# Experts: high parts first in one output column, scatters of a slot together and without order among slots, weight pieces that subtract a PSUM copy

## The chip, the cores and the metric

The kernel runs on one core of a Trainium2 chip. The metric is the device time of one execution in microseconds. TensorE multiplies into PSUM, VectorE and ScalarE split, copy and transpose, GpSimd splits and issues the indirect DMAs, SyncE issues the plain ones.

## The reference

An attention over 8 batches, 8 heads, 576 positions of 64, and behind it a mixture of experts. With `x` the 4608 x 512 rows that the attention gives:

```python
g_idx = np.argmax(x @ w_group, axis=1)             # one of 4 groups
e_idx = np.argmax(xg @ w_expert[g], axis=1)        # one of 4 experts in it
h  = np.maximum(xg[mask_e] @ w1[g, e], 0.0)        # 512 -> 1024
ye = h @ w2[g, e]                                  # 1024 -> 512
out[tok_idx] = combined[:, None] * ye              # combined: product of two softmax weights
```

Each row goes to one of 16 experts, so the rows of `out` that two experts write are distinct.

## The kernel before, in words

The first half of the time (up to about 480 us) is the attention and the routing. The change lies in the second, `moe`. The 16 experts are put in order of their counts and each gets a **slot** of fixed capacity, `CAPS` = 384, 368, 344, 332, 322, 314, 306, 300, 294, 288, 284, 280, 272, 264, 256, 256. Slot 0 is cut into 256 rows and a tile of 128 (`rest`). What doesn't fit is done behind a branch that isn't taken here.

A product in single precision is made of three: every operand is split into a high part in the type fp32r and a low part, the difference, and `h*h`, `h*l` and `l*h` are added in PSUM. So weights have `wh` and `wl`, the input `xh` and `xl`, the hidden rows `hh` and `hl`.

For slots 1 to 15 the loop at the end of `moe` writes the order of TensorE, VectorE and ScalarE out by hand; GpSimd's and SyncE's order is left to a scheduler. In slot k it does:

- **h part**, 8 items (`h_items`): 12 matmuls into one of four accumulators in PSUM, then on ScalarE `hh` (relu), then on VectorE `hl` = max(ph, 0) - hh. Behind item i stands one Z item of the slot before and weight piece i of the slot after.
- **y part**, 4 items (`y_items`), one for each 128 output columns: 24 matmuls, and on ScalarE a copy of the column into `yT`. Ahead of item i stand four X items, two weight pieces and one Z item.

The three lists that are woven in:

- **W**, 16 weight pieces of 128 x 512 of the next slot (`load`): ScalarE makes `wh` from `raw`, then `wl` = raw - wh on VectorE (pieces 0, 4, 8, 10, 12, 14) or on GpSimd (the other ten).
- **X**, the next slot's input (`x_items`): eight items of two VectorE transposes each from `xg` to `xt`, then two that make `xh` (ScalarE) and `xl` (VectorE).
- **Z**, the rows of the slot before (`z_items`): eight items of two VectorE transposes from `yT` to `yr`, then for each 128 rows a `leave`: ScalarE scales the rows by `cw`, GpSimd scatters them to `out` with an indirect DMA. There is one buffer `yr`, so the transposes of a slot into `yr` wait until the scatters of the slot before have landed.

Slots 14 and 15 have a capacity that 128 divides; they multiply straight into rows (`y_rows`) and have no Z of their own. The PSUM pool `pt` has four buffers of 512 columns; in the loop nothing uses it. The weave of the y part is this line:

```python
run(X[4 * i:4 * i + 4] + W[8 + 2 * i:10 + 2 * i] + Z[8 + i:9 + i])
```

so the three `leave`s stand in y items 0, 1 and 2.

## Time and profile before

| | |
|---|---|
| median of 3 runs | 1027.92 us (1026.99 to 1028.95) |
| the profiled execution | 1027.76 us |
| its span, first to last instruction | 1025.7 us |
| busy share of the span: TensorE, VectorE, ScalarE, GpSimd | 88%, 74%, 55%, 55% |
| slots 2 to 13 | 583.4 to 956.6 us |
| mean granted share of TensorE's clock | 0.949 |

Busy shares are averages over parts with different limits; a busy TensorE is not TensorE at its peak. An engine does its instructions in the order of its queue, and the idle time ahead of an instruction is put down to what ended it. A releaser is inferred from semaphores. Line numbers (L953) are those of the kernel before.

### The profile page before, as it was taken

Reading aid. Unit: us, or ns where it says so; the run is one execution under the profiler, and the core shown is the slowest. Engines: PE = TensorE matmul, PEld = TensorE weight load, DVE = VectorE, ACT = ScalarE, POOL = GpSimd, SP = SyncE. Lnnn points to the kernel's source line nnn. Section 1 sums busy time; section 2 is a strip of 40 time slices with the busy share of each in tenths; the row PEclk is TensorE's granted clock in tenths of the full one; section 3 lists DMA queues with packets and bytes.
Section 4 is the critical chain, followed back from the end, with each engine's and each line's share of the span. In section 5 each row is a group of like instructions: output and inputs, shape, how many; then the busy total and the mean of one; then the engine's idle time right before and its main releaser. Section 6 shows DMA issues by size and latency. Waiting matters only on the chain.

```text
span 1025.7 us, 17682 instructions
## 1 busy us (share of the span) xinstructions
PE 900.0 (88%) x5640; PEld 805.6 (79%) x5640; DVE 759.3 (74%) x2023; ACT 569.0 (55%) x1298; POOL 559.6 (55%) x682
## 2 busy tenths in 40 slices
PE   4888999979999999997497999999988998998984
PEld 3777877868788787875387998898888888887873
DVE  7456676866968787866728898878978779888870
ACT  4557675766767676775153454555545454455530
POOL 8434453554636355436277566666656575666630
PEclk9999998999999999998788999999989999999997
DMA  7999999999979899732156444544444544455410
GB/s 201 248 213 235 238 237 224 225 222 225 253 187 247 221 231 226 196 128 68 73 218 200 175 150 164 200 175 149 170 160 163 204 154 158 166 196 193 147 39 21
DMA packets 64164, 187.22 MB, mean 183 GB/s; under 512 B 9628, under 2 KB 18460, under 8 KB 55872
## 3 DMA queue, kind: packets, MB, share of 16 engines
q1 hardware_dynamic: 54768, 166.76, 59.0%
q0 software_dynamic: 7488, 18.89, 5.0%
q8 instruction: 46, 0.75, 0.3%
q10 hardware_dynamic: 1808, 0.37, 0.2%
q14 instruction: 54, 0.44, 0.1%
HBM read 112.12 MB, written 19.69 MB: 129 GB/s over the span
## 4 chain that ended last, share of the span: by engine, by line
PE 52%; DVE 25%; DMA 14%; issue 5%; ACT 2%; POOL 0%; SPq 0%; ACTq 0%; POOLq 0%; DVEq 0%
PE py L1100 12%; PE po L297 11%; PE ph L1045 10%; DVE yr L1138 6%; PE pm L201 4%; DVE wl L953 4%; PE ps L257 4%; PE ps L259 4%; DVE xt L1012 4%; DMA WA<-tl 4%; DVE hl L1041 3%; DMA out_dram<-yr,ids 3%; DMA VT<-in_v_dram 3%; DMA WA<-hl 2%; DVE mx L209 2%
## 5 line engine op out<-in xcount | busy, mean ns | idle before, releaser
L953 POOL TENSOR_TENSOR wl<-raw,wh 128x512 fp32r<-128x512 f32 x166 | 215.9, 1321 | 85.2 <-ACT wh L950 45.0
L209 DVE CUSTOM_DVE_ANT_0 mx<-pm,mask 128x192 bf16<-128x192 f32 (+4 forms) x320 | 127.8, 419 | 63.1 <-PE pm L201 60.7
L1045 PE MATMUL ph<-xh,wh 128*128 128x256 f32 (+13 forms) x512 | 150.3, 312 | 24.3 <-DVE hl L1041 21.1
L950 ACT CAST wh<-raw 128x512 fp32r<-128x512 f32 x256 | 148.1, 616 | 13.4 <-DMA raw<-in_w_dram 13.4
L1045 PE MATMUL ph<-xl,wh 128*128 128x256 f32 (+13 forms) x512 | 149.2, 310 | 1.9 <-DVE xl L1017 1.7
L1100 PE MATMUL py<-hl,wh 128*128 128x256 f32 (+13 forms) x448 | 133.0, 315 | 19.0 <-DVE hl L1041 18.9
L257 PE MATMUL ps<-WA 68*128 68x320 f32 (+4 forms) x384 | 138.7, 365 | 7.7 <-DMA WA<-tl 3.3
L201 PE MATMUL pm<-WA 66*128 66x288 f32 (+4 forms) x384 | 127.8, 364 | 19.2 <-DMA WA<-ch 10.9
L297 PE MATMUL po<-pt,VT 128*128 128x256 f32 (+3 forms) x512 | 125.5, 363 | 17.1 <-DMA VT<-in_v_dram 5.8
L1100 PE MATMUL py<-hh,wh 128*128 128x256 f32 (+13 forms) x448 | 130.8, 310 | 6.3 <-ACT wh L950 6.3
L1138 DVE STREAM_TRANSPOSE yr<-yT 32x384 f32<-32x384 f32 (+1 forms) x208 | 104.6, 503 | 39.4 <-DMA out_dram<-yr,ids 35.2
L1045 PEld LDWEIGHTS ph<-xh,wh 128*128 128x128 f32 x512 | 100.9, 197 | 28.3 <-DVE hl L1041 23.9
L1040 ACT ACTIVATE hh<-ph 128x256 fp32r<-128x256 f32 (+13 forms) x128 | 53.5, 418 | 122.0 <-PE ph L1045 121.3
L276 POOL TENSOR_SCALAR_AFFINE_SELECT pt<-pt 128x128 f32<-128x128 f32 (+2 forms) x192 | 63.7, 339 | 102.9 <-ACT pt L267 99.8
L297 PEld LDWEIGHTS po<-pt,VT 128*128 128x128 f32 x512 | 89.4, 196 | 33.8 <-issue 12.6
L259 PE MATMUL ps<-WB 128*128 128x320 f32 (+4 forms) x384 | 112.3, 305 | 0.0
L1012 DVE STREAM_TRANSPOSE xt<-xg 32x256 f32<-32x256 f32 (+1 forms) x224 | 109.5, 489 | 3.4
L297 PE MATMUL po<-pu,VT 128*128 128x320 f32 (+1 forms) x384 | 109.3, 394 | 0.0
L1100 PEld LDWEIGHTS py<-hl,wh 128*128 128x128 f32 x448 | 87.8, 196 | 25.9 <-DVE hl L1041 25.9
L1045 PEld LDWEIGHTS ph<-xl,wh 128*128 128x128 f32 x512 | 100.9, 197 | 3.7 <-DVE xl L1017 3.0
L953 DVE TENSOR_TENSOR wl<-raw,wh 128x512 fp32r<-128x512 f32 x90 | 90.2, 1004 | 15.2 <-ACT wh L950 13.7
L359 POOL TENSOR_TENSOR xTl<-xT,xTh 128x512 fp32r<-128x512 f32 x30 | 38.2, 1274 | 110.8 <-ACT xTh L355 99.5
(236 smaller groups left out, 1979.6 us busy)
## 6 DMA issues: line engine op xcount, KB each, us to landing
raw<-in_w_dram SPq DMA_DIRECT2D x64, 1024.0 KB
WB<-hl SPq DMA_DIRECT2D x122, 288.0 KB
r<-in_qk_dram SPq DMA_DIRECT2D x32, 576.0 KB
WA<-hl SPq DMA_DIRECT2D x61, 288.0 KB
VT<-in_v_dram SPq DMA_DIRECT2D x32, 480.0 KB
xs<-xr SPq DMA_DIRECT2D x16, 512.0 KB
xs<-xrt SPq DMA_DIRECT2D x8, 128.0 KB
WA<-cumd SPq DMA_DIRECT2D x56, 4.5 KB
```

What stands on the lines that cost most here:

```text
L201: nc.tensor.matmul(ps[:rows, :cw], WA[i][0:66, QA, h, QO + q0:QO + q0 + rows], WA[i][0:66, KA, h, QO + c0:QO + c0 + cw], start=True, stop= ...
L209: nc.vector.tensor_tensor_reduce(out=tmp[:rows, :cw], in0=ps[:rows, :cw], in1=mk[:rows], scale=1.0, scalar=-3.0e38 if c0 == 0 else mo, op0 ...
L257: nc.tensor.matmul(ps[:rows, o:o + w], WA[i][0:68, KA, h, QO + k0:QO + k0 + rows], WA[i][0:68, QA, h, QO + q0:QO + q0 + w], start=True, st ...
L259: nc.tensor.matmul(ps[:rows, o:o + w], WB[p % NBB][:, KA, h, k0:k0 + rows], WB[p % NBB][:, QA, h, q0:q0 + w], start=False, stop=True)
L276: nc.gpsimd.affine_select(out=d, in_=d, pattern=[[0, len(u)], [1, rows]], compare_op=ALU.is_ge, fill=0.0, base=0, channel_multiplier=-1)
L297: nc.tensor.matmul(po[0][:, qa - base:qb - base], VT[p % NVT][:, t, h:h + 2].rearrange("p a d -> p (a d)"), x[:, c:c + qb - qa], start=(j ...
L950: nc.scalar.copy(h[:, j], raw[:, j])
L953: q.tensor_tensor(out=l[:, j], in0=raw[:, j], in1=h[:, j].bitcast(F32), op=ALU.subtract)
L1012: V.transpose(dst[:, 0:n, :, j], src[:, 0:n, :, i])
L1045: nc.tensor.matmul(pss[f][:, :cap], w[f // 4][:, c, (f % 4) * P:(f % 4 + 1) * P], x[:, c, :cap], start=(c == 0 and w is self.w.h and x is ...
L1100: nc.tensor.matmul(pss[c][:, :cap], w[2 + f // 4][:, f % 4, c * P:(c + 1) * P], x[:, f, :cap], start=(f == 0 and w is self.w.h and x is se ...
L1138: V.transpose(dst[:, 0:n, :, i], src[:, 0:n, :, j])
```

## The change

Four edits in `moe`:

1. `scatter` gets a flag that puts it in a group of instructions among which no order is kept. All scatters of slots set it, as they write distinct rows of `out`.
2. In `y_items`, output column 0 of slots 1 to 13 is multiplied in the order high by high, `wl` by `hh`, `wh` by `hl`, eight matmuls each, where before the first and the third alternated.
3. In `load`, the pieces of VectorE are no longer subtracted from `wh`: ScalarE makes a second copy of the same values in a PSUM tile `pw` of the pool `pt`, and VectorE reads that.
4. In the loop, all `leave`s stand ahead of y item 0, in front of X and W.

```diff
--- before.py
+++ after.py
@@ -917,9 +917,13 @@
             return nc.gpsimd.indirect_dma_start(out=xg[:r, t], out_offset=None, in_=xs[0:n], bounds_check=n - 1,
                                          in_offset=bass.IndirectOffsetOnAxis(ap=ids, axis=0), oob_is_err=False)
 
-        def scatter(y, ids):
-            nc.gpsimd.indirect_dma_start(out=out, in_=y, in_offset=None, bounds_check=NTOK - 1, oob_is_err=False,
-                                         out_offset=bass.IndirectOffsetOnAxis(ap=ids, axis=0))
+        def scatter(y, ids, free=False):
+
+            i = nc.gpsimd.indirect_dma_start(out=out, in_=y, in_offset=None, bounds_check=NTOK - 1, oob_is_err=False,
+                                             out_offset=bass.IndirectOffsetOnAxis(ap=ids, axis=0))
+            if free:
+                tc.declare_no_dep(i.ins, group="rows", reason="distinct rows")
+                tc.add_to_no_dep_group("rows", i.ins)
 
         class Expert:
 
@@ -949,8 +953,14 @@
                         with after(tc, hi[i], lo[i]):
                             nc.scalar.copy(h[:, j], raw[:, j])
 
-                            q = nc.gpsimd if j in ((1, 2, 3) if i < 2 else (1, 3)) else eng
-                            q.tensor_tensor(out=l[:, j], in0=raw[:, j], in1=h[:, j].bitcast(F32), op=ALU.subtract)
+                            if j in ((1, 2, 3) if i < 2 else (1, 3)) or eng is not V:
+                                nc.gpsimd.tensor_tensor(out=l[:, j], in0=raw[:, j], in1=h[:, j].bitcast(F32),
+                                                        op=ALU.subtract)
+                                return
+
+                            ps = pt.tile([P, 512], F32R, name=f"pw{self.u}_{i}_{j}", tag="pt")
+                            nc.scalar.copy(ps, raw[:, j])
+                            V.tensor_tensor(out=l[:, j], in0=raw[:, j], in1=ps.bitcast(F32), op=ALU.subtract)
 
                     pieces += [lambda j=j, piece=piece: piece(j) for j in range(4)]
                 return pieces
@@ -1072,7 +1082,7 @@
                                 "p (t d) -> p t d", d=DM)
                         yo = yr[0][:, t]
                         V.tensor_scalar(out=yo, in0=pss[t], scalar1=self.cw[:, t:t + 1], scalar2=None, op0=ALU.mult)
-                        scatter(yo, self.ids[:, t:t + 1])
+                        scatter(yo, self.ids[:, t:t + 1], True)
 
                 return [lambda t=t, f=f: item(t, f) for t in range(len(self.rows)) for f in (0, 4)]
 
@@ -1096,12 +1106,20 @@
                         product(c, self.w.l, self.hh, f)
                     nc.scalar.copy(self.yT[:, c, :cap], pss.pop(c)[:, :cap])
 
-                def product(c, w, x, f):
+                def product(c, w, x, f, stop=None):
                     nc.tensor.matmul(pss[c][:, :cap], w[2 + f // 4][:, f % 4, c * P:(c + 1) * P], x[:, f, :cap],
                                      start=(f == 0 and w is self.w.h and x is self.hh),
-                                     stop=(f == 7 and w is self.w.l))
+                                     stop=(f == 7 and w is self.w.l) if stop is None else stop)
 
                 def item(c):
+                    if c == 0:
+
+                        pss[c] = acc(f"py{u}_{c}")
+                        for w, x in ((self.w.h, self.hh), (self.w.l, self.hh), (self.w.h, self.hl)):
+                            for f in range(8):
+                                product(c, w, x, f, f == 7 and x is self.hl)
+                        nc.scalar.copy(self.yT[:, c, :cap], pss.pop(c)[:, :cap])
+                        return
                     first(c)
                     last(c)
 
@@ -1122,7 +1140,7 @@
                         nc.tensor.transpose(ps[:r, c * P:(c + 1) * P], self.yT[:, c, t * P:t * P + r], ident)
                     yo = yr[:, t]
                     V.tensor_scalar(out=yo[:r], in0=ps[:r], scalar1=self.cw[:r, t:t + 1], scalar2=None, op0=ALU.mult)
-                    scatter(yo[:r], self.ids[:r, t:t + 1])
+                    scatter(yo[:r], self.ids[:r, t:t + 1], True)
 
                 if self.u == 0:
                     return [lambda a=a: item(*a) for a in enumerate(self.rows)]
@@ -1139,7 +1157,7 @@
 
                 def leave(t, r):
                     nc.scalar.mul(yr[:r, t], yr[:r, t], self.cw[:r, t:t + 1])
-                    scatter(yr[:r, t], self.ids[:r, t:t + 1])
+                    scatter(yr[:r, t], self.ids[:r, t:t + 1], True)
 
                 return ([lambda j=j, i=i: turn(j, i) for j in range(4) for i in (0, 2)] +
                         [lambda a=a: leave(*a) for a in enumerate(self.rows)])
@@ -1349,7 +1367,7 @@
                         slots[k + 2].gather()
                 X = slots[k + 1].x_items() if k + 1 < E else []
                 for i, f in enumerate(slots[k].y_items()):
-                    run(X[4 * i:4 * i + 4] + W[8 + 2 * i:10 + 2 * i] + Z[8 + i:9 + i])
+                    run((Z[8:] if i == 0 else []) + X[4 * i:4 * i + 4] + W[8 + 2 * i:10 + 2 * i])
                     f()
                 Z = slots[k].z_items()
             run(Z)
```

How this moves ScalarE, shown in the y part of slot 7 (300 rows), from the first weight copy there. Before (`wh_2`, `wh_3` are the pieces 8 to 15, `yr` the `leave`s, `yT<-py_n` the copy of column n, `xh` the next slot's input):

```order
L950 CAST wh_2_9271<-raw_2_9270 128x512 x2
L1141 ACTIVATE yr_9253<-yr_9253,cws 128x512
L1097 COPY yT<-py_0_9461 128x300
L950 CAST wh_2_9271<-raw_2_9270 128x512 x2
L1141 ACTIVATE yr_9253<-yr_9253,cws 128x512
L1097 COPY yT<-py_1_9503 128x300
L1016 CAST xh_9441<-xt_9443 128x2x294 x2
L950 CAST wh_3_9274<-raw_3_9273 128x512 x2
L1141 ACTIVATE yr_9253<-yr_9253,cws 50x512
L1097 COPY yT<-py_2_9542 128x300
L950 CAST wh_3_9274<-raw_3_9273 128x512 x2
L1097 COPY yT<-py_3_9572 128x300
```

Now the three `leave`s come first, and a copy `pw` stands behind the first of each two pieces:

```order
L1159 ACTIVATE yr_9337<-yr_9337,cws 128x512 x2
L1159 ACTIVATE yr_9337<-yr_9337,cws 50x512
L954 CAST wh_2_9355<-raw_2_9354 128x512
L962 CAST pw_2_0_9554<-raw_2_9354 128x512
L954 CAST wh_2_9355<-raw_2_9354 128x512
L1121 COPY yT<-py_0_9559 128x300
```

And the same y part from the next slot's `xh` to its first `hh` (`ph_0`):

```order
L1026 CAST xh_9529<-xt_9531 128x2x294 x2
L954 CAST wh_3_9358<-raw_3_9357 128x512
L962 CAST pw_3_0_9631<-raw_3_9357 128x512
L954 CAST wh_3_9358<-raw_3_9357 128x512
L1107 COPY yT<-py_2_9636 128x300
L954 CAST wh_3_9358<-raw_3_9357 128x512
L962 CAST pw_3_2_9663<-raw_3_9357 128x512
L954 CAST wh_3_9358<-raw_3_9357 128x512
L1107 COPY yT<-py_3_9668 128x300
L1050 ACTIVATE hh_9717<-ph_0_9719 128x294
```

Between `xh` and `hh` one `leave` has gone and two copies have come.

GpSimd at the same slot, with what each instruction waits for (DMASW are the semaphores of its own DMAs, `yr` the scatters, `xg` the gathers for a later slot). Before:

```order
L953 TENSOR_TENSOR wl_2_9272<-raw_2_9270,wh_2_9271 128x512 [waits PE_49,DMAHW2_49,Activation_49,Pool_49]
L921 DMA out_dram<-yr_9253,ids 4608x512 [waits DMASW7_49,DMASW0_49,Activation_49]
L917 DMA xg_6600<-xs,ids 28x512 [waits DVE_49]
L953 TENSOR_TENSOR wl_2_9272<-raw_2_9270,wh_2_9271 128x512 [waits Activation_49]
L921 DMA out_dram<-yr_9253,ids 4608x512 [waits DMASW0_49,Activation_49]
L917 DMA xg_6600<-xs,ids 128x512 [waits DMASW3_49,DVE_49]
L917 DMA xg_6600<-xs,ids 128x512
L953 TENSOR_TENSOR wl_3_9275<-raw_3_9273,wh_3_9274 128x512 [waits PE_49,DMAHW3_49,Activation_49,Pool_49]
L921 DMA out_dram<-yr_9253,ids 4608x512 [waits DMASW5_49,DMASW2_49,Activation_49]
L953 TENSOR_TENSOR wl_3_9275<-raw_3_9273,wh_3_9274 128x512 [waits Activation_49]
```

Now:

```order
L957 TENSOR_TENSOR wl_1_9353<-raw_1_9351,wh_1_9352 128x512 [waits PE_49,DMAHW1_49,Activation_49,Pool_49]
L957 TENSOR_TENSOR wl_1_9353<-raw_1_9351,wh_1_9352 128x512 [waits Activation_49] x2
L922 DMA out_dram<-yr_9337,ids 4608x512 [waits DMASW0_49,Activation_49]
L922 DMA out_dram<-yr_9337,ids 4608x512 [waits DMASW1_49,Activation_49]
L917 DMA xg_6600<-xs,ids 28x512 [waits DMASW2_49,DVE_49]
L922 DMA out_dram<-yr_9337,ids 4608x512 [waits DMASW3_49,Activation_49]
L957 TENSOR_TENSOR wl_2_9356<-raw_2_9354,wh_2_9355 128x512 [waits PE_49,DMAHW2_49,Activation_49,Pool_49]
L957 TENSOR_TENSOR wl_2_9356<-raw_2_9354,wh_2_9355 128x512 [waits Activation_49]
L917 DMA xg_6600<-xs,ids 128x512 [waits DMASW4_49,DVE_49]
L917 DMA xg_6600<-xs,ids 128x512 [waits DMASW5_49]
```

The scatters stand in front of the pieces of `wl_2`, with one gather between the second and the third, and each waits for one DMA semaphore and ScalarE.

TensorE at output column 0 of slot 7. Before, `hh` and `hl` take turns, and go on so for 16 matmuls:

```order
L1045 MATMUL ph_7_9422<-xh_9096,wl_1_8924 128x300 x4
L1100 MATMUL py_0_9461<-hh_9276,wh_2_8926 128x300
L1100 MATMUL py_0_9461<-hl_9277,wh_2_8926 128x300
L1100 MATMUL py_0_9461<-hh_9276,wh_2_8926 128x300
L1100 MATMUL py_0_9461<-hl_9277,wh_2_8926 128x300
```

Now:

```order
L1055 MATMUL ph_7_9510<-xh_9172,wl_1_8996 128x300 x4
L1110 MATMUL py_0_9559<-hh_9360,wh_2_8998 128x300 x4
L1110 MATMUL py_0_9559<-hh_9360,wh_3_9001 128x300 x4
L1110 MATMUL py_0_9559<-hh_9360,wl_2_8999 128x300 x4
L1110 MATMUL py_0_9559<-hh_9360,wl_3_9002 128x300 x4
L1110 MATMUL py_0_9559<-hl_9361,wh_2_8998 128x300 x4
L1110 MATMUL py_0_9559<-hl_9361,wh_3_9001 128x300 x4
L1110 MATMUL py_1_9599<-hh_9360,wh_2_8998 128x300
```

The first `hl` is read by the seventeenth matmul instead of the second.

## Rows read from the trace of the kernel before

**Rows 1.** The first line of the profile's page.
```profile
span 1025.7 us, 17682 instructions
```

**Rows 2.** TensorE in order of time, at the start of slot 2's h part (344 rows), in the y part of slot 13 (264 rows), at the start of slot 14 and of slot 15's second matmul. Columns: start in us, us, engine, line, operation, operands, shapes, count and, in brackets, idle time before it with what ended it. The length of a matmul is modelled and overlaps the next one; the distance between two starts is what it takes.
```profile
583.42 0.32 PE L1045 MATMUL ph<-xh,wh 128*128 128x344 f32 x1
583.58 0.32 PE L1045 MATMUL ph<-xl,wh 128*128 128x344 f32 x1
...
942.02 0.28 PE L1100 MATMUL py<-hh,wh 128*128 128x264 f32 x1
942.14 0.28 PE L1100 MATMUL py<-hl,wh 128*128 128x264 f32 x1
...
956.58 0.28 PE L1045 MATMUL ph<-xh,wh 128*128 128x256 f32 x1
...
986.78 0.58 PE L1045 MATMUL ph<-xl,wh 128*128 128x256 f32 x1 [0.95 <-DVE xl L1017]
```

**Rows 3.** What TensorE waited for in slots 2 to 13 (583.4 to 956.6): us in total, times, the longest.
```profile
PE py L1100 <- DVE hl L1041: 18.9, 26, 1.2
PE ph L1045 <- DVE hl L1041: 12.9, 8, 3.3
```

**Rows 4.** Slot 7 and what lies beside it, as a stretch of 34 us: its length, then busy time of TensorE, its weight loads, VectorE, ScalarE and GpSimd with their instruction counts, the granted share of TensorE's clock, DMA share and GB/s.
```profile
740.00:774.00 34.00, 30.68 (x198) 30.08 (x198) 26.32 (x50) 16.49 (x35) 20.18 (x17) 0.90 0.46 161
```

**Rows 5.** What VectorE waited for in slots 2 to 13: us in total, times, the longest.
```profile
DVE yr L1138 <- DMA out_dram<-yr,ids: 33.9, 11, 5.8
DVE wl L953 <- ACT wh L950: 11.3, 12, 1.0
```

**Rows 6.** VectorE in order of time, from the first `hl` of slot 7 (300 rows) to the first `hl` of slot 8 (294 rows) and the `yr` turn behind it; columns as in rows 2.
```profile
743.63 0.47 DVE L1041 SCALAR_TENSOR_TENSOR hl<-ph,hh 128x300 fp32r<-128x300 f32 x1
749.91 1.15 DVE L1138 STREAM_TRANSPOSE yr<-yT 32x384 f32<-32x384 f32 x2 [5.81 <-DMA out_dram<-yr,ids]
751.09 0.69 DVE L953 TENSOR_TENSOR wl<-raw,wh 128x512 fp32r<-128x512 f32 x1
...
763.03 4.66 DVE L1012 STREAM_TRANSPOSE xt<-xg 32x384 f32<-32x384 f32 x8
767.71 0.81 DVE L953 TENSOR_TENSOR wl<-raw,wh 128x512 fp32r<-128x512 f32 x1
768.54 3.59 DVE L1012 STREAM_TRANSPOSE xt<-xg 32x256 f32<-32x256 f32 x8
772.16 0.69 DVE L953 TENSOR_TENSOR wl<-raw,wh 128x512 fp32r<-128x512 f32 x1
772.88 1.45 DVE L1017 TENSOR_TENSOR xl<-xt,xh 128x588 fp32r<-128x588 f32 x2
774.25 0.68 DVE L953 TENSOR_TENSOR wl<-raw,wh 128x512 fp32r<-128x512 f32 x1
775.94 1.16 DVE L953 TENSOR_TENSOR wl<-raw,wh 128x512 fp32r<-128x512 f32 x1 [1.01 <-ACT wh L950]
777.08 0.47 DVE L1041 SCALAR_TENSOR_TENSOR hl<-ph,hh 128x294 fp32r<-128x294 f32 x1
779.83 1.15 DVE L1138 STREAM_TRANSPOSE yr<-yT 32x384 f32<-32x384 f32 x2 [2.29 <-DMA out_dram<-yr,ids]
```

**Rows 7.** GpSimd in order of time, y part of slot 7: the three scatters of slot 6's rows.
```profile
764.09 1.03 POOL L921 DMA_INDIRECT out_dram<-yr,ids  x1 [0.40 <-ACT yr L1141]
...
768.80 1.03 POOL L921 DMA_INDIRECT out_dram<-yr,ids  x1 [0.84 <-DMA out_dram<-yr,ids]
...
776.74 1.21 POOL L921 DMA_INDIRECT out_dram<-yr,ids  x1 [0.20 <-ACT yT L1097]
```

**Rows 8.** Line 921, the scatters of the whole run.
```profile
DMA to landing us min/median/max: 2.0/3.2/6.5
```

**Rows 9.** ScalarE in order of time, from the next slot's `xh` to its first `hh`; L950 is the copy of a weight piece (two in a row), L1141 the last `leave`, L1097 a column of y out of PSUM.
```profile
772.16 1.27 ACT L1016 CAST xh<-xt 128x588 fp32r<-128x588 f32 x2 [4.69 <-DVE xt L1012]
773.34 1.13 ACT L950 CAST wh<-raw 128x512 fp32r<-128x512 f32 x2
774.38 0.72 ACT L1141 ACTIVATE yr<-yr,cws 50x512 f32<-50x512 f32 x1
775.00 0.38 ACT L1097 COPY yT<-py 128x300 f32<-128x300 f32 x1
...
776.64 0.41 ACT L1040 ACTIVATE hh<-ph 128x294 fp32r<-128x294 f32 x1
```

**Rows 10.** VectorE's weight pieces in slots 2 to 13 as a group: busy us, mean ns of one, then idle time before them with what ended it.
```profile
L953 DVE TENSOR_TENSOR wl<-raw,wh 128x512 fp32r<-128x512 f32 x71 | 67.5, 951 | 12.7 <-ACT wh L950 11.3
```

**Rows 11.** Line 1041, the `hl` of all slots: count, then ns of one, least, median and most, and the time of the first and the last.
```profile
L1041 DVE SCALAR_TENSOR_TENSOR hl<-ph,hh x128: 406/458/542, 488.9 to 1000.4; 128x256 fp32r<-128x256 f32 x24, 128x368 fp32r<-128x368 f32 x8, 128x344 fp32r<-128x344 f32 x8, 128x332 fp32r<-128x332 f32 x8
```

**Rows 12.** VectorE in order of time, the start of slot 14's h part.
```profile
961.99 1.15 DVE L1138 STREAM_TRANSPOSE yr<-yT 32x384 f32<-32x384 f32 x2 [1.29 <-DMA out_dram<-yr,ids]
963.16 3.06 DVE L953 TENSOR_TENSOR wl<-raw,wh 128x512 fp32r<-128x512 f32 x1
```

**Rows 13.** VectorE in order of time, the h part of slot 1: a weight piece and the scan over the slots.
```profile
545.36 4.29 DVE L953 TENSOR_TENSOR wl<-raw,wh 128x512 fp32r<-128x512 f32 x1
...
550.20 4.29 DVE L1310 TENSOR_TENSOR_SCAN incl<-need,zero 128x32 f32<-128x32 f32 x1
```

**Rows 14.** TensorE in order of time, at the same place.
```profile
554.98 0.68 PE L1045 MATMUL ph<-xh,wh 128*128 128x368 f32 x1 [6.00 <-DVE hl L1041]
```

## The prediction

> **What bounds the kernel now.** I read the span first, then TensorE in order of time, then the waits of TensorE and of VectorE, then one slot of VectorE, ScalarE and GpSimd in order of time. The profiled execution took 1027.76 us: 1025.7 of span [rows 1] and 2.1 around it; the median of three runs is 0.16 above it. Less than 0.2% (2 us) can't be told from no change.
>
> Slots 2 to 13 run from 583.42 to 956.58, 373.2 us. Their matmuls follow each other at 0.16 us in slot 2 and 0.12 in slot 13 [rows 2]; a slot has 192, so 30.7 and 23.0, on average 26.9, and TensorE alone would need 322. [...] VectorE itself waits 33.9 us for the out-DMA, in 11 of the 12 slots, and 11.3 for ScalarE's `wh` [rows 5].
>
> In slot 7 [rows 6] VectorE makes `hl` of item 0 at 743.63, then wants to turn back slot 6's rows into `yr`, and stands for 5.81 us, since slot 5's last rows have not left `yr`. From 749.91 it runs without a pause to 772.16, where the last `xt` turn ends (call this S), and the next slot's `hl` starts at 777.08. One slot is 33.45 us from `hl` to `hl`, and TensorE's 192 matmuls, 26.9 at a distance between those two (0.14), would have fitted. Why is `yr` late? The third `leave` stands in y item 2, behind `xh`, which waits for all of X: its scatter starts at 776.74 [rows 7], a landing takes 2.0 to 6.5, median 3.2 us [rows 8], and at 779.83 the next slot waits again.
>
> **The change, part by part.**
>
> *Leaves together.* The last Z turn ends at 763.0. ScalarE then does three `leave`s at 0.62 each (774.38 to 775.00 [rows 9]), up to 764.9. Now the second scatter waits for the landing of the first [rows 7]; without that, and with about 1 us each, the scatters issue at 764, 765 and, with one gather that stands ahead of the third and waits for the first four X turns (2.3 us), at about 768. The slowest landing of 6.5 brings that to 775.6. The next turn into `yr` stands 5.84 us behind S (below), at 778.0: 2.4 us to spare. So the whole 33.9 us go. What the step is moved past: on ScalarE pieces 8 and 9; piece 8's two copies are ready at about 766.1, VectorE wants them after eight turns at 767.7, so that is covered by 1.6 us (without the cover it would cost what it lacks, once a slot). On GpSimd pieces 9 and 11, whose `wl` is first read a whole h part later.
>
> *Copies in PSUM.* Six pieces a slot gain a ScalarE copy. Two copies start 1.04 us apart from what follows them [rows 9], 0.52 each: 3.1 us a slot more on ScalarE, which is busy for 16.5 of 34 [rows 4]. What counts is the two behind `xh`, because `hh` of the next item 0 stands behind them in ScalarE's queue: from S to that `hh` is 4.48 us now (772.16 to 776.64), less the `leave` that moves away (0.62), plus two copies (1.04): 4.90. `hl` starts 0.44 later and takes 0.50, so the next `yr` turn starts at S + 5.84 instead of S + 5.42: 0.42 worse a slot, 5.0 in twelve. No trace row has a ScalarE copy into PSUM. Bounds: half and double of 0.52, that is 6 us less or 13 more over the loop; I take the copy it resembles, the same columns from the same source. The four buffers of `pt` are free in the loop, and ScalarE runs at most two pieces ahead.
>
> On the gain side: VectorE's pieces take 0.951 on average over 71, where an undisturbed one takes 0.69 [rows 6, 10], 18.5 us in all. The long ones, up to 4.29 [rows 13], lie beside GpSimd's pieces, and have both operands in SBUF; the `hl` instructions, one operand in PSUM and one in SBUF, take 0.41 to 0.54 in all 128 cases [rows 11], beside the same GpSimd work. I take it that the new form loses the tail too. 2.4 of the 18.5 belong to a piece that slot 1 began, and about 5.3 are the last piece of each slot (1.16 in rows 6), which is inside the 4.92 from S to `hl` already and so inside the 0.42. That leaves 10.8. If nothing of it goes, 10.8 less gain.
>
> Does VectorE pay for the PSUM operand? `hl` at 300 columns takes 0.47, a piece at 512 takes 0.69 [rows 6]: 0.22 for 212 columns, 1.04 ns a column, and a remainder of 0.16 for both. So nothing. [...]
>
> *High parts first in column 0.* TensorE asks for `hl` 16 matmuls later than now. In slot 7's new rhythm, measured from S: `xl` is ready and the h part starts at 1.44, it ends at 14.9; VectorE ends the last `hl` at about 17.9. The old order wants it at 17.0, the new one at 18.1 (it also wants the last `hh` at 15.9, and ScalarE has it at 15.6). But y ends at 28.3 and the next `xh`, `xl` are there only at 27.9 + 1.44: TensorE would wait a microsecond there anyway. I cost the edit at nothing; its cover is that VectorE sets the pace. Where TensorE does (slots 2 and 3) it saves up to 1 us.
>
> *The loop.* With the waits gone, VectorE needs 22.1 from the first `yr` turn to S (749.91 to 772.16 less 0.12) and 5.84 on: 27.9 for slot 7, above TensorE's 26.9. In slots 2 to 4 both are near 30. So: 373.2 - 33.9 - 10.8 + 5.0 = 333.5, which is 39.7 less.
>
> *Around it.* Slot 14: a wait of 1.29 and a piece of 3.06 [rows 12], less 0.42: 3.3 less up to 986.78. From there to the end TensorE sets the pace and nothing changes. Slot 1: a piece and a scan of 4.29 each [rows 13] hold up `hl`, and TensorE waits 6.00 [rows 14]. The piece should take 0.69; against that ScalarE has four more copies ahead of `hh`, 2 us. Between 0 and 9 with the clock, I take 4. For dips of the clock after TensorE's waits at each slot's start I add 2, as 1.5 us between `hh` and `hl` absorb most of one.
>
> Sum: 1027.76 - 39.7 - 3.3 - 4 + 2 = **982.8**, so 983.
>
> **Rivals.**
> - *TensorE sets the pace.* If the copies cost half and the new order pays, the loop comes down towards 322 and slot 1 gives all 9: some 970. For it: the two paces lie 1 us apart. Against it: the queue from `xh` to `hh` is fixed by the order.
> - *The wait stays in part.* In about half the slots a gather stands ahead of the third scatter. If it, or a slow landing, brings the third scatter back to where it was, six waits of 3.1 stay: 19 us, 1002.
> [...]
> - *The other waits go on.* The scatters still wait for each other through something else, and `yr` comes free no sooner: 1024 to 1030, no change.
> - *Slower.* The two copies between `xh` and `hh` are the place. The change loses once they add more than 45 us over 13 slots, 3.5 a slot: each would have to take over 2.3 us instead of 0.52, say because ScalarE has to wait for a `pt` buffer that VectorE frees late; at 2.6 each, 1035. Against it: in the rhythm above VectorE waits for these copies, so the buffers come back at once.
>
> **How the numbers follow.** Forecast 0.55, TensorE's pace 0.12, wait in part 0.20, PSUM price 0.05, no change 0.03, slower 0.05. Faster: 0.55 + 0.12 + 0.20 + 0.05 = 0.92; the same 0.03; slower 0.05. The range reaches from 968, a little under TensorE's pace, to 1004, a little over the wait in part, and leaves out what is less than 2 in 10.
>
> **What would show it.** Right: no wait of `yr` for the out-DMA; three scatters in one group behind the last Z turn; pieces on VectorE at 0.69 throughout; 27 to 28 us from `hl` to `hl` at slot 7; VectorE waiting for the copies behind `xh`; TensorE's waits at the start of h, for `xh` and `xl`. Wrong: the waits of `yr` stay (scatters late), the new copy is longer than 0.6 us, or ScalarE waits for `pt`.

## The result and the profile after

The changed kernel takes 982.89 us (median of 4 runs, 980.08 to 985.53) where the kernel before took 1027.64 (4 runs): a ratio of 0.9575, 95% interval 0.9534 to 0.9616. The forecast was 983.0 with a range of 968 to 1004.

The first line of the page, beside [rows 1]:

```profile
span 981.5 us, 17865 instructions
```

VectorE in order of time, from the first `hl` of slot 7 to that of slot 8, beside [rows 6] (start, length, engine, line, operation, operands, shapes, count, idle time before it):

```profile
731.17 0.47 DVE L1051 SCALAR_TENSOR_TENSOR hl<-ph,hh 128x300 fp32r<-128x300 f32 x1 [0.50 <-ACT hh L1050]
731.56 1.14 DVE L1156 STREAM_TRANSPOSE yr<-yT 32x384 f32<-32x384 f32 x2
...
753.68 0.69 DVE L963 TENSOR_TENSOR wl<-raw,pw 128x512 fp32r<-128x512 f32 x1
754.40 1.45 DVE L1027 TENSOR_TENSOR xl<-xt,xh 128x588 fp32r<-128x588 f32 x2
756.04 0.69 DVE L963 TENSOR_TENSOR wl<-raw,pw 128x512 fp32r<-128x512 f32 x1 [0.19 <-issue]
757.85 0.69 DVE L963 TENSOR_TENSOR wl<-raw,pw 128x512 fp32r<-128x512 f32 x1 [1.12 <-ACT pw L962]
759.03 0.46 DVE L1051 SCALAR_TENSOR_TENSOR hl<-ph,hh 128x294 fp32r<-128x294 f32 x1 [0.49 <-ACT hh L1050]
759.41 1.14 DVE L1156 STREAM_TRANSPOSE yr<-yT 32x384 f32<-32x384 f32 x2
```

The turn into `yr` follows `hl` at once, where it stood for 5.81 us before. From `hl` to `hl` it is 27.86 instead of 33.45. VectorE now waits for ScalarE's copies and for `hh` (1.12 and 0.49).

ScalarE at the same place, beside [rows 9], and GpSimd's three scatters with the gather among them, beside [rows 7]:

```profile
753.68 1.27 ACT L1026 CAST xh<-xt 128x588 fp32r<-128x588 f32 x2 [3.28 <-DVE xt L1022]
...
757.23 0.59 ACT L962 CAST pw<-raw 128x512 fp32r<-128x512 f32 x1
757.76 0.62 ACT L954 CAST wh<-raw 128x512 fp32r<-128x512 f32 x1
758.28 0.40 ACT L1107 COPY yT<-py 128x300 f32<-128x300 f32 x1
758.58 0.42 ACT L1050 ACTIVATE hh<-ph 128x294 fp32r<-128x294 f32 x1
```

```profile
745.72 1.03 POOL L922 DMA_INDIRECT out_dram<-yr,ids  x1 [2.36 <-ACT yr L1159]
747.06 1.00 POOL L922 DMA_INDIRECT out_dram<-yr,ids  x1 [0.31 <-issue]
748.36 0.98 POOL L917 DMA_INDIRECT xg<-xs,ids  x1 [0.30 <-ACT wh L954]
749.65 0.96 POOL L922 DMA_INDIRECT out_dram<-yr,ids  x1 [0.30 <-ACT pw L962]
```

All three issue within 4 us; the third stood 12.65 behind the first before. The copy into PSUM starts 0.53 us ahead of the next instruction.

VectorE's pieces as one line of the program (count, then ns of one: least, median, most), what VectorE waited for in slots 2 to 13, beside [rows 5], and what TensorE waited for there, beside [rows 3]:

```profile
L963 DVE TENSOR_TENSOR wl<-raw,pw x90: 656/687/692, 526.1 to 942.7; 128x512 fp32r<-128x512 f32 x90
```

```profile
DVE wl L963 <- ACT pw L962: 12.4, 11, 1.2
DVE hl L1051 <- ACT hh L1050: 8.4, 13, 2.8
DVE wl L963 <- issue: 1.7, 8, 0.3
```

```profile
PE ph L1055 <- DVE xl L1027: 2.7, 7, 0.4
PE py L1110 <- DVE hl L1051: 2.0, 5, 0.9
PE ph L1055 <- ACT xh L1026: 1.7, 4, 0.6
```

No piece is longer than 0.692, the wait of `yr` is gone, and TensorE's waits for `hl` fell from 31.8 to 2.0. Slots 2 to 13 as one stretch, before and after (length, busy time of TensorE, its weight loads, VectorE, ScalarE, GpSimd, granted share of the clock, DMA):

```profile
583.42:956.58 373.16, 340.32 (x2305) 329.49 (x2305) 315.84 (x574) 189.87 (x390) 233.25 (x186) 0.97 0.48 171
```

```profile
583.79:914.04 330.25, 323.66 (x2306) 318.48 (x2305) 297.08 (x573) 222.68 (x461) 226.48 (x186) 1.00 0.54 192
```

The stretch lost 42.9 of the 44.2 us that the span lost. VectorE's busy time fell by 18.8 (2.3 of it a piece that slot 1 began in the kernel before and that ran to 585.76 us), its idle time by 24.2.

### The profile page after: what moved, and what is told of

Read it like the earlier page. It is cut to its first block, busy times and chain, and to the rows that moved or that the text cites. A ratio compares the mean times of both kernels' runs of the same rounds, so it can differ in the third digit from the quotient of the medians.

```text
span 981.5 us, 17865 instructions
## 1 busy us (share of the span) xinstructions
PE 882.4 (90%) x5640; PEld 792.3 (81%) x5640; DVE 739.4 (75%) x2023; ACT 611.5 (62%) x1388; POOL 549.3 (56%) x682
## 5 line engine op out<-in xcount | busy, mean ns | idle before, releaser
L957 POOL TENSOR_TENSOR wl<-raw,wh 128x512 fp32r<-128x512 f32 x166 | 213.7, 1301 | 79.8 <-ACT wh L954 59.5
L954 ACT CAST wh<-raw 128x512 fp32r<-128x512 f32 x256 | 155.5, 616 | 15.4 <-DMA raw<-in_w_dram 13.4
L1055 PE MATMUL ph<-xh,wh 128*128 128x256 f32 (+13 forms) x512 | 147.4, 307 | 7.1 <-ACT xh L1026 4.0
L1110 PE MATMUL py<-hh,wh 128*128 128x256 f32 (+13 forms) x448 | 115.2, 306 | 6.3 <-ACT wh L954 6.3
L1110 PE MATMUL py<-hl,wh 128*128 128x256 f32 (+13 forms) x448 | 115.3, 305 | 2.0 <-DVE hl L1051 2.0
L297 PE MATMUL po<-pu,VT 128*128 128x320 f32 (+1 forms) x384 | 111.3, 399 | 0.0
L201 PEld LDWEIGHTS pm<-WA 66*128 66x128 f32 (+1 forms) x384 | 70.8, 196 | 41.8 <-DVE mc L209 17.8
L145 POOL TENSOR_TENSOR hl<-r,hl 128x576 fp32r<-128x576 f32 x62 | 88.0, 1421 | 5.6 <-ACT hl L142 3.2
```

The lines of the kernel that those rows point to most:

```text
L145: (nc.vector if p < 1 else nc.gpsimd).tensor_tensor(out=hl[:, 2 + part], in0=r[:, part], in1=hl[:, part].bitcast(F32), op=ALU.subtract)
L201: nc.tensor.matmul(ps[:rows, :cw], WA[i][0:66, QA, h, QO + q0:QO + q0 + rows], WA[i][0:66, KA, h, QO + c0:QO + c0 + cw], start=True, stop= ...
L297: nc.tensor.matmul(po[0][:, qa - base:qb - base], VT[p % NVT][:, t, h:h + 2].rearrange("p a d -> p (a d)"), x[:, c:c + qb - qa], start=(j ...
L954: nc.scalar.copy(h[:, j], raw[:, j])
L957: nc.gpsimd.tensor_tensor(out=l[:, j], in0=raw[:, j], in1=h[:, j].bitcast(F32), op=ALU.subtract)
L1055: nc.tensor.matmul(pss[f][:, :cap], w[f // 4][:, c, (f % 4) * P:(f % 4 + 1) * P], x[:, c, :cap], start=(c == 0 and w is self.w.h and x is ...
```

## The experiments

The whole time of one kernel moves by some 10 us from run to run. Part of that is the attention half, which the edits don't touch: slot 0's first matmul stands anywhere from 474.3 to 484.8 us in the fourteen traces. Each ratio is to the kernel before, run beside that kernel on the same chip; the medians of different rows can come from different chips. So each kernel is read by its **loop**, from the first matmul of slot 2 to that of slot 14 in its profiled execution. The loop of the changed kernel came out as 330.25 and 330.21 in two traces. The table has the loop, the waits of `yr` for the out-DMA in it, and the time by which VectorE's pieces exceed 0.69, both summed from slot 2's first `hl` to slot 14's.

| kernel | median us | ratio to before (95%) | loop | waits of `yr` | excess of pieces |
|---|---|---|---|---|---|
| before | 1027.64 | 1 | 373.2 | 33.9 | 16.2 |
| changed | 982.89 | 0.9575 (0.9534 to 0.9616) | 330.2 | 0 | 0 |
| changed, without PSUM copies | 1004.79 | 0.9778 (0.971 to 0.9847) | 359.6 | 0 | 47.5 |
| changed, old order in column 0 | 979.55 | 0.9526 (0.9459 to 0.9593) | 330.7 | 0 | 0 |
| changed, leaves apart | 1010.27 | 0.9841 (0.9764 to 0.9917) | 361.3 | 23.5 | 0 |
| changed, scatters ordered | 1015.67 | 0.9898 (0.9819 to 0.9976) | 357.7 | 26.4 | 0 |
| before, with PSUM copies alone | 1011.33 | 0.9875 (0.9799 to 0.995) | 362.5 | 22.6 | 0 |
| changed, copies behind `xh` doubled | 994.43 | 0.9756 (0.9667 to 0.9845) | 343.8 | 0 | 0 |
| changed, pieces 12 and 14 from `wh` | 985.49 | 0.9619 (0.9543 to 0.9694) | 338.4 | 0 | 26.2 |

**The copies in PSUM taken away.**

```diff
...
-                            ps = pt.tile([P, 512], F32R, name=f"pw{self.u}_{i}_{j}", tag="pt")
-                            nc.scalar.copy(ps, raw[:, j])
-                            V.tensor_tensor(out=l[:, j], in0=raw[:, j], in1=ps.bitcast(F32), op=ALU.subtract)
+                            q = nc.gpsimd if j in ((1, 2, 3) if i < 2 else (1, 3)) else eng
+                            q.tensor_tensor(out=l[:, j], in0=raw[:, j], in1=h[:, j].bitcast(F32), op=ALU.subtract)
```

> The changed kernel without the copies in PSUM (VectorE's pieces read wh again). Theory A, the prediction's: in slots 2 to 13 of the changed kernel no piece of VectorE is longer than 0.69, where the kernel before had 16.2 us of excess over 0.69 in them; this excess comes back, less the two copies behind xh (S, the end of the last xt turn, to the next hh 4.34 instead of 4.90). Loop 8 us longer than the changed kernel's 330.3, slot 14 two to three longer, slot 1 unchanged or two shorter: 989 to 994 us in all. Rival B: TensorE covers the tails, 983 to 985. Rival C: the copies cost more on ScalarE than they save on VectorE, 972 to 978.

The loop came out 29.3 longer, not 8. There is no wait of `yr`, but VectorE's pieces now average 1.384 us where they averaged 0.951 in [rows 10]. The excess of 47.5 did not count in full: VectorE's other waits are 17.0 shorter than in the changed kernel (15.3 against 32.3, from slot 2's first `hl` to slot 14's). First the group in slots 2 to 13, then VectorE's last piece ahead of slot 8's first `hl` and GpSimd beside it:

```profile
L957 DVE TENSOR_TENSOR wl<-raw,wh 128x512 fp32r<-128x512 f32 x71 | 98.3, 1384 | 6.0 <-ACT wh L954 4.6
```

```profile
768.25 3.02 DVE L957 TENSOR_TENSOR wl<-raw,wh 128x512 fp32r<-128x512 f32 x1 [0.40 <-ACT wh L954]
771.20 0.45 DVE L1045 SCALAR_TENSOR_TENSOR hl<-ph,hh 128x294 fp32r<-128x294 f32 x1
...
768.18 2.54 POOL L957 TENSOR_TENSOR wl<-raw,wh 128x512 fp32r<-128x512 f32 x2
```

The piece starts with a run of two GpSimd pieces and ends 0.55 behind it; `hl`, one operand in PSUM, takes 0.45. In the kernel before GpSimd did this beside the same piece, which took 1.16 [rows 6]:

```profile
775.25 1.30 POOL L953 TENSOR_TENSOR wl<-raw,wh 128x512 fp32r<-128x512 f32 x1
...
777.97 5.00 POOL L953 TENSOR_TENSOR wl<-raw,wh 128x512 fp32r<-128x512 f32 x4
```

Between the first piece and the run of four stood the third scatter (776.74 in [rows 7]), and VectorE's piece ended 0.55 behind the first one, at 777.10. With the scatters moved ahead GpSimd's pieces close up to a run. Theory A had the mechanism and priced it from a trace in which GpSimd's work lay elsewhere.

**Column 0 in the old order.** The branch for `c == 0` is not taken.

> The changed kernel with column 0 in the old order of products. Theory A: nothing, 983 to 985. In slot 7 the last hl ends 2.8 us after the y part starts; the old order wants it at its sixteenth matmul, 2.1 after the start, so TensorE would wait 0.7 in the y part and 0.4 less for xl at the next h start, while VectorE's rhythm of 27.9 stays. Rival B: each stall counts and takes the clock down with it, 12 times 0.7 to 1.5 us: 991 to 1001.

The loop took 330.7 against 330.2. What TensorE waited for in it:

```profile
PE py L1110 <- DVE hl L1051: 7.4, 12, 0.9
PE ph L1055 <- DVE xl L1027: 0.2, 1, 0.2
```

TensorE waits 5.4 us more in the y part and 4.2 less at the starts of h (2.7 and 1.7 above): nearly the same wait at another place. Theory A holds, the edit is worth nothing here.

**Leaves apart, scatters free.**

```diff
-                    run((Z[8:] if i == 0 else []) + X[4 * i:4 * i + 4] + W[8 + 2 * i:10 + 2 * i])
+                    run(X[4 * i:4 * i + 4] + W[8 + 2 * i:10 + 2 * i] + Z[8 + i:9 + i])
```

> The changed kernel with the three leaves back in y items 0, 1 and 2; the scatters stay without order. Theory A: the third leave stands behind xh and three copies, ends 3.4 us after S, its scatter issues at about S + 4.5 and lands 3.2 later, near S + 8; the next yr turn is due at S + 6.3. A wait of 1.5 to 2.5 in nearly every slot, and 0.6 more of ScalarE's queue ahead of hh: 1005 to 1015 us. Rival B: the order among scatters was the cause and not their place; freed of it they land in time and the time stays under 990.

The median is 1010.27, as theory A has it. In slot 7 `xh` starts at 762.16 (S, the end of the last `xt` turn), the third leave at 764.89, its scatter at 766.74 (S + 4.6); the next `yr` turn, due at 768.58, starts at 769.75. As long as the leave stands behind `xh`, the freedom from order is worth 1.2 us of the loop (362.5 to 361.3, below).

**Scatters ordered, leaves together.** The flag does nothing (`if False` in place of `if free`).

> The changed kernel with the scatters ordered again, the three leaves still together. Theory A: the second scatter waits for the first one's landing (3.2 us), the third for the second one's, so in slot 7 they issue at about 745.7, 750 and 754.5 and the last lands near 758.7, before the yr turn at 759.4: hidden at the median landing, up to 3 us where a landing is slow. 983 to 993 us. Rival B: order among the scatters was the main cause, the 34 us of waits come back in good part: above 1005.

Rival B holds: 26.4 us of waits came back. But GpSimd hardly waits for a landing (1.1 us in all, once). GpSimd in order of time, y part of slot 7:

```profile
759.47 1.03 POOL L922 DMA_INDIRECT out_dram<-yr,ids  x1 [4.24 <-ACT yr L1159]
761.03 0.97 POOL L917 DMA_INDIRECT xg<-xs,ids  x1 [0.54 <-DVE xt L1022]
762.11 1.29 POOL L957 TENSOR_TENSOR wl<-raw,wh 128x512 fp32r<-128x512 f32 x1
763.90 1.29 POOL L957 TENSOR_TENSOR wl<-raw,wh 128x512 fp32r<-128x512 f32 x1 [0.51 <-ACT wh L954]
765.35 1.03 POOL L922 DMA_INDIRECT out_dram<-yr,ids  x1 [0.16 <-issue]
767.65 1.07 POOL L917 DMA_INDIRECT xg<-xs,ids  x1 [1.26 <-DVE xt L1022]
769.03 1.44 POOL L917 DMA_INDIRECT xg<-xs,ids  x1 [0.31 <-ACT xh L1026]
770.77 0.98 POOL L922 DMA_INDIRECT out_dram<-yr,ids  x1 [0.30 <-issue]
```

GpSimd's order is a scheduler's. With an order to keep it put the second scatter behind a gather and two pieces, and the third behind two gathers, the first of which waits for VectorE's `xt` turns (0.30 or 0.31 stands between two DMAs of GpSimd here, whether ScalarE's `xh` or nothing is named behind it). All three `leave`s are done by 760.4, yet the third scatter issues at 770.77, behind the `xh` of the next slot, as in the kernel before. So the flag acts mainly through the order of GpSimd's program.

With the PSUM copies in place the four combinations of these two edits give loops of 362.5 (neither), 361.3 (free alone), 357.7 (together alone) and 330.2 (both). The first of these is the next kernel, which also has column 0 in the old order.

**The PSUM copies alone, on the kernel before.** Edits 1, 2 and 4 undone.

> The kernel before with the copies in PSUM alone: scatters ordered, leaves in y items 0 to 2, column 0 in the old order. Theory A: the wait of yr hangs on the third leave, which stands behind xh; the pieces lose their 16 us of excess, but the two copies put the leave 1.04 later behind S, so the scatter, its landing and the next yr turn too, twelve times 1.04 = 12.5 us. About nothing is left: 1018 to 1030. Rival B: the gains of the edits add up; what the copies give beside the other edits (the kernel without them took 1004.8 instead of 982.9), 22 us, they give here too: 1001 to 1010.

Neither holds: the loop is 10.7 shorter, the time 1011.33. From slot 2's first `hl` to slot 14's the excess of 16.2 went, VectorE's other waits rose by 14.9 (24.6 to 39.5) and those of `yr` fell by 11.3. Theory A erred in the scatter. Only one of the two copies stands ahead of the third leave, which starts 2.73 behind S instead of 2.22; and the scatter still issues at S + 4.58 (775.28 with S at 770.70, as 776.74 with 772.16 before), since GpSimd's own queue sets it (a piece of 1.30 goes ahead). `yr` came free no later, while the turn that wants it was due about a microsecond later.

**The two copies behind `xh` made twice.**

```diff
                             nc.scalar.copy(ps, raw[:, j])
+                            if i == 3:
+                                nc.scalar.copy(ps, raw[:, j])
```

> The changed kernel with two more ScalarE copies a slot: the copies into PSUM of pieces 12 and 14, the two behind xh, are made twice. Theory A: the queue from S to the next hh is on the path, 4.90 becomes 5.94, and VectorE's rhythm grows by 1.04 in each slot from 4 on (in slots 2 and 3 it has up to 2 us of other waits that take it): 10 to 12.5 us in the loop, 2 around it: 993 to 998. Rival B: TensorE sets the pace, and the copies disappear in ScalarE's idle time: 982 to 986.

The loop is 13.6 longer: theory A, a little over its bound. A copy repeated into the same buffer took 0.62 us from start to start, not 0.52, so from S to `hh` it is 6.17 on average instead of 4.93. VectorE's rhythm from `hl` to `hl` is 1.22 to 1.26 longer in every slot. TensorE's slots 2 and 3 keep their 30.29 and 28.82 us, and the time is paid from slot 4 on. What ScalarE has more to do between `xh` and `hh` was paid nearly in full (13.6 of 14.9).

**Pieces 12 and 14 from `wh`.** Their copies are left out, `ps = h[:, j]`.

> The changed kernel in which pieces 12 and 14, the two behind xh, are subtracted from wh in SBUF, without their copies; the other four keep theirs. Theory A: ScalarE's queue from S to hh gets 1.04 shorter, but VectorE's piece 14, with both operands in SBUF, starts beside a run of two GpSimd pieces (2.54) and ends with it, as it did in the kernel with no copies at all (3.02): S to hl 6.1 instead of 5.35, the loop about 9 us longer, slot 14 likewise: 988 to 996. Rival B: ScalarE's queue is what counts, S to hl 4.3, and the loop comes down until TensorE sets the pace: 972 to 978.

The loop is 8.2 longer, as theory A has it, though the median of 985.49 lies below its 988. ScalarE's queue from S to `hh` is a microsecond shorter (3.98 on average, 4.93 with all copies), but VectorE's piece 14 is held again, 3.01 us in slot 7, and `hl` starts 5.99 behind S on average instead of 5.38.

**Copies of pieces 12 and 13 ahead of `xh`,** VectorE's piece 12 still behind `xl` (`late` holds it back):

```diff
...
+                    if i == 2:
+                        xw = W[12:14] + X[8:10] + [lambda: wts[k + 1].late[0]()] if W else []
+                    elif i == 3:
+                        xw = W[14:16] + [lambda: wts[k + 1].late[2]()] if W else []
...
```

> The changed kernel with ScalarE's copies of pieces 12 and 13 (two wh, one pw) ahead of the next slot's xh instead of behind it; VectorE's and GpSimd's work stays in its order. ScalarE stands idle for 3.3 us ahead of xh in slot 7 of the changed kernel. Theory A: these copies go into that idle time, S to hh becomes 3.3 instead of 4.9, VectorE's idle time of 2.7 a slot falls to about 1.3, and TensorE sets the pace in nearly all slots: loop 322 to 325 instead of 330.3, in all 974 to 979. Rival B: a buffer or the weights are not there by then, ScalarE waits and xh gets late: 983 to 990.

The median is 967.59 and the loop 320.3, both below theory A's ranges. It was run again, beside the changed kernel and two tries at slot 1, on one chip:

> The changed kernel once more, beside the two tries to better it. Theory: slots 2 to 13 take 330 to 331 us again, since nothing in them is left to chance but the DMA; the start of slot 0, ahead of every edit, has been anywhere from 474 to 485 us in the traces so far, and the whole time moves with it: 976 to 988.

> The kernel with ScalarE's copies of pieces 12 and 13 ahead of xh, beside the changed kernel on one chip. Theory A: the loop again 320 to 321 us, slots 14 and 15 with 2 to 3 less as well: 10 to 14 us below the changed kernel in the medians. Rival B: most of the gain seen was the early start of slot 0 (475.9): under 6 us.

| kernel | median us (6 runs) | ratio to before (95%) | loop | slot 1 |
|---|---|---|---|---|
| changed, again | 982.81 | 0.9544 (0.9478 to 0.9609) | 330.2 | 48.1 |
| copies of 12 and 13 early | 971.11 | 0.9477 (0.9434 to 0.952) | 319.9 | 48.0 |
| no GpSimd pieces in slot 1's h part | 976.96 | 0.9506 (0.9461 to 0.9551) | 330.2 | 47.4 |
| both | 967.54 | 0.944 (0.9395 to 0.9486) | 319.9 | 47.4 |

Theory A's direction holds: 11.7 us less in the medians (9.6 without the two longest runs of the changed kernel, 985.03 and 984.55), 10.3 of it in the loop. ScalarE from the copies to the first `hh` of slot 8, then all that TensorE waited for in the loop:

```profile
748.70 0.59 ACT L962 CAST pw<-raw 128x512 fp32r<-128x512 f32 x1
749.22 0.62 ACT L954 CAST wh<-raw 128x512 fp32r<-128x512 f32 x1
751.56 1.27 ACT L1031 CAST xh<-xt 128x588 fp32r<-128x588 f32 x2 [1.72 <-DVE xt L1027]
...
755.46 0.42 ACT L1055 ACTIVATE hh<-ph 128x294 fp32r<-128x294 f32 x1 [0.45 <-PE ph L1060]
```

```profile
PE ph L1060 <- DVE xl L1032: 0.4, 1, 0.4
```

The copies lie in time in which ScalarE stood idle, `hh` waits for TensorE instead of the other way round, and TensorE sets the pace: it waits 0.4 us in all, so 319.9 is about what slots 2 to 13 come to with these matmuls.

**Slot 1 without GpSimd's pieces in its h part.** Six pieces go to VectorE, with copies.

```diff
-                            if j in ((1, 2, 3) if i < 2 else (1, 3)) or eng is not V:
+                            if eng is not V or j in ((1, 2, 3) if i < 2 else (1, 3)) and (self.u != 2 or i > 1):
```

> The changed kernel in which, in slot 1's h part alone, VectorE does the six pieces of GpSimd too, each with its copy in PSUM. Theory A: the three long ones there (need 2.69, scan 3.22, xts 3.34) are held by GpSimd's runs of two pieces; without those they take 0.18, 0.4 to 0.7 and 0.75, TensorE's waits of 3.25 and 3.03 shrink, and slot 1 takes 44 to 48 us instead of 50.9, although VectorE has 4.1 us more to do: 3 to 6 us less than the changed kernel. Rival B: they are long whatever GpSimd does, slot 1 stays at 50 or rises to 55 with the extra pieces and copies.

> Both of the last two edits in the changed kernel. Theory A: they touch different stages and add up: loop 320 to 321, slot 1 at 44 to 48, 13 to 20 us less than the changed kernel. Rival B: without slot 1's gain, the same as the kernel with early copies.

Slot 1 of the changed kernel first, VectorE and under it GpSimd:

```profile
539.97 2.69 DVE L1316 TENSOR_TENSOR need<-csl,low 128x32 f32<-128x32 f32 x1
...
543.32 3.22 DVE L1328 TENSOR_TENSOR_SCAN incl<-need,zero 128x32 f32<-128x32 f32 x1
...
548.91 3.34 DVE L1348 TENSOR_TENSOR xts<-idl,idf 128x576 f32<-128x576 f32 x1
...
540.07 2.53 POOL L957 TENSOR_TENSOR wl<-raw,wh 128x512 fp32r<-128x512 f32 x2
...
543.93 2.52 POOL L957 TENSOR_TENSOR wl<-raw,wh 128x512 fp32r<-128x512 f32 x2
...
549.08 2.54 POOL L957 TENSOR_TENSOR wl<-raw,wh 128x512 fp32r<-128x512 f32 x2
```

And with the edit:

```profile
543.44 2.68 DVE L1316 TENSOR_TENSOR need<-csl,low 128x32 f32<-128x32 f32 x1
...
546.78 3.25 DVE L1328 TENSOR_TENSOR_SCAN incl<-need,zero 128x32 f32<-128x32 f32 x1
...
552.40 0.74 DVE L1348 TENSOR_TENSOR xts<-idl,idf 128x576 f32<-128x576 f32 x1
...
543.52 2.54 POOL L957 TENSOR_TENSOR wl<-raw,wh 128x512 fp32r<-128x512 f32 x2
...
547.39 2.55 POOL L957 TENSOR_TENSOR wl<-raw,wh 128x512 fp32r<-128x512 f32 x2
```

Two of the three runs are slot 1's own last pieces, which the edit left on GpSimd, and the two instructions beside them stay as long as they were. The third run is gone, and its instruction takes 0.74. That is the mechanism, shown within one kernel: 2.68 and 3.25 us beside runs of 2.54 and 2.55, 0.74 without one where it was 3.34. What slot 1 gains stays open: it took 47.4 us, against 48.1 and 50.9 in the two traces of the changed kernel, and those two differ in the granted clock (below). Whether the whole time gains can't be told from these intervals. Both edits together have the lowest median, 967.54, but their interval overlaps that of the early copies alone.

## Why the prediction was right, and where it was not

The total was right, by a sum in which errors of opposite sign cancel, and that 983 met the median to 0.1 us is luck. On the spans: attention and slot 0 2.4 less, slot 1 2.8 more, the loop 42.9 less, slot 14 up to slot 15's second matmul 3.2 less, the rest 1.6 more. The 2.4 of the attention half is chance, since no edit touches it.

- **Leaves together, -33.9.** Right as a difference: the whole wait is gone, and the scatters issue 1.1, 2.4 and 5.0 behind the last Z turn (744.63), as forecast (1, 2, 5). But the reason given for the second scatter, the landing of the first, was the smaller part. What matters is where the scheduler puts the scatters on GpSimd, and with the copies in place neither edit alone is worth more than 5 us.
- **Pieces, -10.8.** Right against the trace of before, wrong as what the edit is worth. Without the copies the rest of the change takes the loop to 359.6, 13.6 less, not 33.9, because the excess grows to 47.5. The step that failed took the excess from a trace in which GpSimd's pieces lay elsewhere, and never asked where they would lie after the scatters had moved.
- **Two more copies between `xh` and `hh`, +5.0.** Right: S to `hh` 4.90 (753.68 to 758.58) as forecast, the copy into PSUM 0.52 from start to start, S to the `yr` turn 5.73 instead of 5.84. That this queue is on the path, from slot 6 on, is shown from both sides, by the doubled and by the early copies.
- **No price for the PSUM operand.** Right: 687 ns median, at most 692, over 90 pieces with one operand in PSUM and one in SBUF, against 0.69 for an undisturbed piece with both in SBUF. No run shows the price that has 0.05 among the chances.
- **High parts first, 0.** Right, and for the reason given.
- **The loop, 333.5.** Measured 330.25. By VectorE's rows from slot 2's first `hl` to slot 14's, the waits of `yr` gave 33.9 and the pieces 16.0, as counted (10.8 + 5.3), but its other waits grew by 7.7 (24.6 to 32.3) where 5.0 + 5.3 were counted. That is 2.6 of the difference of 3.2. Slot 7 was forecast at 27.9 and took 27.86. In slots 2 to 5 TensorE waits for nothing and takes the same time, within 0.02 us, as with the copies early: there it sets the pace, where the sum let VectorE set it. From slot 6 on the slots are 0.4 to 2.0 us longer than with the copies early, and the queue from `xh` to `hl` sets the pace.
- **Slot 1, -4.** Wrong: 50.87 instead of 48.09, and 48.06 in the second trace. The piece does take 0.66 now, but `need` and `xts`, which follow, take 2.69 and 3.34 instead of 0.18 and 0.75. Both have two operands in SBUF and lie beside a run of two GpSimd pieces (2.53 and 2.54), so here taking one out moved the wait on. The two traces are 2.8 us apart, and the granted share of the clock differs: from 555 to 568 us it is 0.77 in the first (0.50 up to 561, where four matmuls take 1.43 us instead of 0.83) and 1.00 in the second, from 535 to 555 it is 0.98 in the first and 0.91 in the second. TensorE's two longest waits are 3.25 and 3.03 us in the first, both ahead of 555, and 3.2 and 1.4 in the second. Whether the copies pay in slot 1 is open: without them it took 45.9, in the traces with them 46.7 to 50.9.
- **Clock dips, +2.** Wrong: the granted share in the loop rose from 0.97 to 1.00. In stretches of 1 us it fell to 0.50 six times in the loop of the kernel before, around or behind TensorE's waits for `hl` (for 6.8 us in slot 7, around the end of the wait of 3.3, and for 3.4 us each of the other times), and in the changed kernel's loop never under 0.99. So the trace of the changed kernel does not show the 2.
- **Slot 14, -3.3.** Right (30.20 to 26.96). Behind it "nothing changes" was off: 38.9 became 40.5, of which the second trace has 1.1 less (37.8 to 40.5 in the fourteen traces); the cause was not tested.

Of the rivals, that TensorE sets the pace is what one further edit brings. That changes within 0.2% can be told apart was too hopeful: the runs of one kernel here lie 0.2 to 2% apart.

## What to carry to other kernels

Price an edit at where the other engines' work will lie after it: here the copies alone took 11 us off the loop and the other edits 14 without them, but all together 43, since with the scatters moved VectorE's pieces beside GpSimd's are held longer (an excess of 47.5 us instead of 16.2), and the copies take that away (0). When a flag frees instructions from an order, look at what the scheduler does with them, not only at the wait. When one instruction of a queue is held by another engine, ask which instruction behind it can be held in its place.

## What the runs showed of the hardware

In these traces VectorE's pieces, `need`, the scan and `xts`, all with both operands in SBUF, were held, with the exceptions below, by GpSimd's pieces that ran beside them, even if they take 0.18 us otherwise (`need`: 0.18 in the kernel before, 2.69 beside a run of 2.53 in the changed one). In the kernel before, all 33 pieces of VectorE from slot 2 on that take over 0.72 us end 0.55 or 0.56 us behind the end of a GpSimd piece. Beside a run of two, without the copies, a piece did not get through between them (3.02 beside 2.54). With one operand in PSUM none of 90 is held (0.692 at most), though 53 of them overlap a piece of GpSimd. The order of the recorded starts alone does not tell which of the two is held. In the kernel before, seven pieces of VectorE that start 0.11 to 0.46 us ahead of a GpSimd piece keep their 0.69, and that GpSimd piece takes 1.38 to 1.75 instead of 1.29. But another that starts 0.35 ahead is held (2.21 at 987.24 us), without the copies so are some that start 0.21 to 0.49 ahead (3.62 at 876.03 us), and so is `need`, 0.10 ahead of its run in the changed kernel (starts on GpSimd are rough).

In the changed kernel a 512-column copy on ScalarE takes 584 ns into PSUM (median of 90) and 615 into SBUF (median of 256).
